# The order of all steps of a planned kernel comes from a stored string, and two-bank steps take neighbouring banks

## The chip, the cores and the metric

One core of a Trainium2 chip. The number is the device time of one execution in microseconds (us). The kernel before was run three times.

## The reference

An attention block with 32 inducing vectors, and a gated feed-forward layer on its result. With `B, N, C = 4, 12416, 128`, `M = 32`, `DFF = 1536`:

```python
def mab(q, kv):
    s = scale * (q @ kv.transpose(0, 2, 1))
    a = np.exp(s - s.max(-1, keepdims=True))
    a /= a.sum(-1, keepdims=True) + 1e-09
    return a @ kv
h = mab(I, x)                     # I: the inducing vectors, per batch
y = mab(x, h).reshape(B * N, C)
gate = np.maximum(y @ w_gate, 0.0)
out = (gate * (y @ w_val)) @ w_out
```

## The kernel before

Batch 0's first attention runs in `first_batch`, written out by hand. Everything after it is a list of 1454 steps (`Op`): 751 on TensorE, 216 on ScalarE, 344 on VectorE, 65 on GpSimd, 78 on the sync engine. A step has a name, an engine, a duration that the planner assumes, the steps that it depends on, a number of PSUM banks that it takes or frees, and a function that emits its instructions. `Plan.order` lays the steps out in time by that model; the kernel then emits them in that order, so that each engine receives its instructions in the planned order and works through them in that order. The waits in the program come from the tiles that the instructions read and write, not from the planner.

What a batch b consists of:

- `prepare` (b = 1 to 3): `ld` loads of x (GpSimd queue), `turn` transposes (TensorE, with `xT` copies on VectorE, or by DMA on the sync queue for the pairs in `BY_DMA`), `s1a`/`s1b` scores, `p1` exponentials (ScalarE), `ha`/`hb` sums over tokens, `hs`, `hsum`, `zs` to `hT` small steps.
- `second_scores`: `S` scores against h, copied out by `Sc` (VectorE).
- `tables`: `g1`/`g2` gates, products `U` (VectorE), tables `T` (TensorE, 24 matmuls a step) and their copies `Tc`, and the same for `u5`, `T5`.
- `quadratic`: 48 `e` scores (TensorE, two matmuls of 512 columns), each with one exponential `f` of 128x1024 (ScalarE) into a ring of six `F` buffers of four; 48 output tiles `o`, each in two halves a and b. A unit is three tiles: `o..a` of its first takes two banks; a reciprocal `r` and a product `d` (VectorE, into `osb`) read both banks, and `d` frees them; every second unit is stored (`st`). There are 16 units in a batch, 64 in all.
- `check`: `far` sums of squares on GpSimd, `v`, `diag`, `vp`, `eps`, then `test`, twelve small GpSimd instructions. At the very end `tot`, `totp`, `left` and `load` turn the four tests into the condition of the branch to a general kernel.

PSUM has eight banks. Banks 0 to 3 are two double ones for `e`, `s1` and the like ("E"). Banks 4 to 7 are four single ones ("D"), numbered 0 to 3. A step that needs two D banks gets the two that came free first, whichever they are, and addresses them with

```python
def dbanks(o):
    a, b = o.got
    return AL[:, 4 + a : 5 + b : b - a, :]
```

In the plan of the kernel before, 113 steps take two banks: 40 of them (0,1) or (2,3), 27 (1,2), and 46 a pair with a gap: 25 (0,3), 11 (0,2), 10 (1,3). Of the units, the first eight of batch 2 (o2.0 to o2.23) alternate between (0,1) and (2,3); the last ten of batch 3 (o3.18 to o3.47) alternate between (1,3) and (0,2).

In the plan before, `pick` chooses at each moment, per engine, the step with the earliest latest start, by due times (`goal`, `LAG`) and boosts; exponentials come out in the order of their number.

Of the kernel before, what the change touches and what calls it, by code (L numbers as in the profile page):

```python
# [18 lines left out]
BOOST_FREE = 30.0  # L19
BOOST_PE = 6.0  # L20
# [8 lines left out]
BY_DMA = {(2, 1), (2, 3), (2, 5), (3, 1), (3, 3), (3, 5)}  # L29


class Op:
    __slots__ = (
        "name", "eng", "dur", "post", "deps", "emit", "take", "frees", "goal", "dma",
        "succ", "last", "start", "end", "seen", "got", "left", "first", "prev", "tail", "fixed", "boost",
# [3 lines left out]
class Plan:  # L39


    TOL = {"PE": 0.12, "ACT": 0.2, "DVE": 0.3}
    BANKS = {"E": 2, "D": 4}

# [3 lines left out]
    def op(self, name, eng, dur, emit, deps=(), post=None, take=None, frees=(), goal=1e9, dma=0.0):  # L48
# [10 lines left out]
        o.succ, o.got, o.fixed, o.boost = [], None, None, BOOST_FREE if o.frees and eng == 'DVE' else 0.0  # L59
# [11 lines left out]
    def order(self, begin):  # L71
        ops = self.ops
        for o in ops:
            for d, lat in o.deps:
                d.succ.append((o, lat))
            o.left = len(o.deps)
        for o in reversed(ops):
            o.last = o.goal - o.dur
            for s, lat in o.succ:
                o.last = min(o.last, s.last - self.lag(o, s, lat) - o.dur - o.dma)  # L80
        for o in ops:
            o.last -= o.boost
        free = dict.fromkeys(("PE", "ACT", "DVE", "POOL", "SP"), 0.0)
        free.update(begin)
        slots = {k: [0.0] * n for k, n in self.BANKS.items()}
        ready = {e: [] for e in free}
        for o in ops:
            if not o.left:
                ready[o.eng].append(o)
        server = free.pop("DMA", 0.0)  # L90
        done = []

        def est(o):
            if o.fixed is not None:
                return 0.0
            t = free[o.eng]
            for d, lat in o.deps:
                t = max(t, d.seen - d.post + self.lag(d, o, lat))
            if o.take:
                kind, n = o.take  # L100
                times = sorted(s for s in slots[kind] if s is not None)
                if len(times) < n:
                    return None
                t = max(t, times[n - 1])
            return t

        def pick(e):
            c = [(t, o) for o in ready[e] for t in [est(o)] if t is not None]
            if not c:
                return None  # L110
            base = min(t for t, _ in c)
            t, o = min(((t, o) for t, o in c if t <= base + 0.03), key=lambda a: a[1].last)
            tol = self.TOL.get(e)
            soon = [(u, v) for u, v in c if v.last < o.last and u < t + o.dur - tol] if tol else []
            if soon:
                u, v = min(soon, key=lambda a: a[1].last)
                fit = [(w, p) for w, p in c if w + p.dur <= u + tol]
                if fit:
                    t, o = min(fit, key=lambda a: a[1].last)
                else:  # L120
                    t, o = u, v
            return t, o

        while any(ready.values()):
            best = None
            for e in ready:
                p = pick(e)
                if p and (best is None or p[0] < best[0]):
                    best = p
            assert best, [(e, [o.name for o in r][:5]) for e, r in ready.items()]  # L130
            t, o = best
            ready[o.eng].remove(o)
            o.start = t
            o.end = t + o.dur
# [8 lines left out]
            if o.take:  # L143
                kind, n = o.take
                s = slots[kind]
                avail = sorted((i for i in range(len(s)) if s[i] is not None and s[i] <= t + 1e-9), key=lambda i: (s[i], i))
                o.got = sorted(avail[:n])
                assert len(o.got) == n
                for i in o.got:
                    s[i] = None  # L150
# [4 lines left out]
            for s, _ in o.succ:  # L155
                s.left -= 1
                if not s.left:
                    ready[s.eng].append(s)
        assert len(done) == len(ops)
        return sorted(done, key=lambda o: o.start)  # L160

# [9 lines left out]
def quadratic_body(ctx, tc, x, inducing, moe_w_gate, moe_w_val, moe_w_out, out):  # L171
# [390 lines left out]
    def prepare(b):  # L562
        s = state[b]
        s["turn"], s["load"] = {}, {}
        for q in (NQ, *range(NQ)):
# [13 lines left out]
            if q < NQ and (b, q) not in BY_DMA:  # L579
# [20 lines left out]
                s["turn"][q] = op(f"xT{b}.{q}", "DVE", 1.15, copy, frees=[o])  # L600
# [21 lines left out]
        for u in range(NQ // 2):  # L622
# [64 lines left out]
            def add(u=u, o=ha):  # L687
# [16 lines left out]
            [s["h"]],  # L704
        )
        zs = op(
            f"zs{b}", "DVE", 0.19,
# [4 lines left out]
            [hs],  # L712
        )
        o = op(f"zp{b}", "PE", 0.5, None, [zs], take=("D", 1))
        o.emit = lambda o=o: pe.matmul(dbank(o)[:, 0:M], ones32, small["zs"], start=True, stop=True)
        zc = op(
            f"zk{b}", "DVE", 0.15, lambda o=o: dve.tensor_copy(out=zk, in_=dbank(o)[:, 0:M]),
# [5 lines left out]
            f"h{b}", "DVE", 0.15,  # L723
# [7 lines left out]
            f"hc{b}", "DVE", 0.13,  # L731
# [7 lines left out]
                f"hT{b}", "DVE", 0.13,  # L739
# [5 lines left out]
    def second_scores(b):  # L745
# [5 lines left out]
        war = [*state[b - 2]["e_last"], state[b - 2]["far"]] if b >= 2 else []  # L751
        for u in range(4):
# [28 lines left out]
            d = op(f"Sc{b}.{u}", "DVE", 1.2 if u < 3 else 0.2, out_, war, frees=[o])  # L781
            s["Sd"].append(d)

        s["F5"] = []
        for v in range(2):
# [11 lines left out]
            o.emit = mm5  # L797
            k = len(f5_done)
# [18 lines left out]
    def tables(b):  # L817
# [23 lines left out]
        def gv(k):  # L841
# [9 lines left out]
            [o2],  # L851
# [9 lines left out]
        def value_out(to, lo, n):  # L861
# [7 lines left out]
        vw = op(f"vw{b}", "DVE", 0.33, lambda: value_out(M, 0, NS), [o2, *free_g])  # L869
        gw = op(f"gw{b}", "DVE", 0.33, lambda: gate_out(M, 0, NS), [m, *free_g])  # L870
        sc = op(
            f"sums{b}", "DVE", 0.15,
# [6 lines left out]
            f"mags{b}", "DVE", 0.5,  # L879
# [10 lines left out]
        def odd(src, dst):  # L890
            dve.tensor_copy(out=dst[:, :, 0 : G - 1], in_=src[:, :, 1:G])

        vo = op(f"vb{b}", "DVE", 0.4, lambda: odd(va, vb), [vv, vw])
        go = op(f"gb{b}", "DVE", 0.4, lambda: odd(ga, gb), [g, gw])
# [3 lines left out]
            f"u5a{b}", "DVE", 0.3,  # L898
# [6 lines left out]
            f"u5b{b}", "DVE", 0.3,  # L905
# [102 lines left out]
        def mm5(step, o):  # L1008
            ps = dbanks(o1_)

            def mm(k, half, t):
# [13 lines left out]
                f"T5c{b}", "DVE", 0.65,  # L1025
# [11 lines left out]
    def check(b):  # L1037
# [8 lines left out]
        for k in range(4):  # L1046
            part = flat[:, 768 * k : 768 * k + 768]
            steps.append((1.7, Z if k else A, part, part, mul))
            if k:
                steps.append((1.7, A, A, Z, add))  # L1050
# [4 lines left out]
        for k, (dur, dst, in0, in1, f) in enumerate(steps):  # L1055
# [13 lines left out]
            f"v{b}", "DVE", 0.5,  # L1069
# [10 lines left out]
            [vm],  # L1080
        )
        o = op(f"vp{b}", "PE", 0.6, None, [dg], take=("D", 1))
        o.emit = lambda: pe.matmul(dbank(o)[:, 0:P], ones32, diag, start=True, stop=True)
        ep = op(
            f"eps{b}", "DVE", 0.25,
            lambda: dve.tensor_reduce(out=eps, in_=dbank(o)[:, 0:P], axis=AX.X, op=ALU.max),  # L1086
            frees=[o],
        )
        lo = op(
            f"zlo{b}", "DVE", 0.13,  # L1090
            lambda: dve.tensor_reduce(out=small["zlo"], in_=zk, axis=AX.X, op=ALU.min),
            [s.get("zk")], goal=late,
        )
        hi = s["zcheck"] = op(
            f"zhi{b}", "DVE", 0.13,
# [25 lines left out]
    def quadratic(b):  # L1121
        s = state[b]
        s["e_last"], s["o_all"] = [], []
# [3 lines left out]
        def rest():  # L1127
# [11 lines left out]
            s["e_last"].append(o)  # L1139

            def exp(o=o):
# [7 lines left out]
                f"fr{b}", "ACT", 0.6, exp, state[b - 1].get("o_rest", []) if b else [],  # L1149
# [12 lines left out]
            def out2():  # L1162
# [16 lines left out]
                f"dr{b}", "DVE", 0.25,  # L1179
# [12 lines left out]
        def scores(xb):  # L1192
# [3 lines left out]
            for j in range(4):  # L1196
# [10 lines left out]
                if xb == NX - 1:  # L1207
                    s["e_last"].append(o)
# [8 lines left out]
        units = {}  # L1217

        def outputs(p):
# [48 lines left out]
            if tt == TPB - 1:  # L1268
                f_done[k] = [o2]
# [86 lines left out]
    for o in plan.ops:  # L1356
        if o.eng == "PE" and o.take is None and not o.name.startswith("e"):
            o.boost = BOOST_PE
        if o.name.startswith("r"):
            o.boost = BOOST_FREE  # L1360
# [253 lines left out]
```

## Time and profile before

| what | value |
|---|---|
| median of 3 runs | 370.79 us (367.03 to 372.0) |
| profiled execution, its own time | 374.55 us |
| its span | 372.8 us |
| mean granted TensorE clock | 0.905 of 2.4 GHz |
| busy: TensorE, ScalarE, VectorE, GpSimd | 280.8, 216.3, 181.2, 86.9 us |

The span runs from the first to the last instruction of the profiled execution; 1.75 us of its own time lie around it. It is 1.0% above the median of the runs. Busy time of TensorE counts the last part of a matmul's passage through the array too, so that it is not work at its peak.

### The profile page before, as it was taken

How to read it: one execution, taken by the hardware profiler on the slowest of the kernel's cores; microseconds unless marked ns; L12 is line 12 of the kernel's file. 1: busy time of each engine (PE TensorE's matmuls, PEld its weight loads, DVE VectorE, ACT ScalarE, POOL GpSimd, SP SyncE). 2: the span in 40 equal slices, each digit the busy share in tenths (PEclk: the TensorE clock that was granted, in tenths of full speed). 3: DMA queues.
4: the chain of work that ended last, by engine and by line, in shares of the span. 5: the costliest groups of instructions: out<-in, count | busy, mean ns of one | idle time of the engine just before them, and what ended most of it. 6: DMA issues, size and time to landing. Idle time of an engine off the chain costs nothing.

```text
span 372.8 us, 15723 instructions
## 1 busy us (share of the span) xinstructions
PE 280.8 (75%) x7251; PEld 208.8 (56%) x7251; DVE 181.2 (49%) x383; ACT 216.3 (58%) x248; POOL 86.9 (23%) x146
## 2 busy tenths in 40 slices
PE   5796889874779687778758889997878878767740
PEld 2672577664456465446637558876555657544430
DVE  4559856550337922344224796642368443432330
ACT  3456887952668154677522996785558454548600
POOL 3663076002300050080101007600020500061011
PEclk9699899995789998999957999998789999989985
DMA  8999963318972412252534443440202204422230
GB/s 302 384 158 215 212 126 155 156 44 196 214 164 86 122 28 86 86 142 96 142 62 130 151 96 60 169 184 4 88 2 86 88 4 191 160 84 86 88 152 28
DMA packets 30042, 46.85 MB, mean 126 GB/s; under 512 B 16624, under 2 KB 17296, under 8 KB 29968
## 3 DMA queue, kind: packets, MB, share of 16 engines
q1 hardware_dynamic: 25056, 35.04, 26.7%
q0 software_dynamic: 4864, 10.72, 15.8%
q8 instruction: 58, 0.95, 1.1%
q14 instruction: 16, 0.13, 0.1%
q10 hardware_dynamic: 48, 0.02, 0.0%
HBM read 27.80 MB, written 25.43 MB: 143 GB/s over the span
## 4 chain that ended last, share of the span: by engine, by line
PE 62%; DVE 17%; ACT 10%; issue 7%; POOL 1%; DVEq 0%; POOLq 0%; ACTq 0%
PE AL L1257 32%; ACT F L1211 9%; PE AL L1201 9%; DVE osb L1290 7%; PE AL L977 6%; PE AL L664 2%; PE AL L631 2%; DVE S L777 2%; DVE xT L596 2%; PE xT_ps L372 2%; PE AL L586 1%; DVE rzo L1285 1%; DVE U L933 1%; PE warm_ps L290 1%; PE AL L1012 1%
## 5 line engine op out<-in xcount | busy, mean ns | idle before, releaser
L1211 ACT ACTIVATE F<-AL 128x1024 f16<-128x1024 f32 x192 | 184.5, 1031 | 100.8 <-PE AL L1201 96.7
L1257 PE MATMUL AL<-T,F 64*128 64x129 f16 x3456 | 148.7, 228 | 30.0 <-DVE osb L1290 20.9
L1257 PEld LDWEIGHTS <-F 64*128 64x128 f16 x3456 | 115.5, 99 | 65.3 <-issue 33.9
L1201 PE MATMUL AL<-S,pairs 64*128 64x512 f16 x384 | 77.8, 402 | 14.0 <-ACT F L1211 11.2
L1290 DVE TENSOR_TENSOR osb<-AL,rzo 128x768 f32<-128x768 f32 x64 | 61.0, 954 | 8.7 <-PE AL L1257 7.6
L1285 DVE RECIPROCAL rzo<-AL 128x6 f32<-128x6 f32 x64 | 12.4, 195 | 102.7 <-PE AL L1257 94.7
L1061 POOL TENSOR_TENSOR far<-S 128x768 f16<-128x768 f16 x16 | 25.6, 1610 | 137.9 <-DVE U L933 81.4
L1201 PEld LDWEIGHTS <-pairs 64*128 64x128 f16 x384 | 23.3, 97 | 26.9 <-issue 22.8
L977 PE MATMUL AL<-wo,U 64*128 64x128 f16 x768 | 25.8, 216 | 4.1 <-DVE osb L1290 1.5
L977 PEld LDWEIGHTS <-U 64*128 64x128 f16 x768 | 22.9, 94 | 9.0 <-issue 5.9
L1061 POOL TENSOR_TENSOR far<-far 128x768 f16<-128x768 f16 (+2 forms) x20 | 25.0, 1249 | 1.6
L242 POOL DMA_DIRECT2D x<-in_x_dram x18 | 9.8, 555 | 50.2 <-PE AL L664 39.9
L596 DVE COPY xT<-AL 128x2048 f16<-128x2048 f16 x12 | 14.7, 1221 | 7.5 <-PE AL L586 6.9
L1101 POOL TENSOR_SCALAR eps<-eps 128x1 f32<-128x1 f32 x4 | 0.8, 189 | 70.3 <-DVE eps L1086 58.9
L645 ACT ACTIVATE p<-AL 128x1024 f16<-128x1024 f32 x9 | 9.2, 1023 | 12.7 <-PE AL L631 12.5
L631 PE MATMUL AL<-indT,xT 64*128 64x32 f16 x576 | 11.1, 175 | 5.9 <-issue 5.4
L777 DVE CAST S<-AL 128x1024 f16<-128x1024 f32 x12 | 14.6, 1214 | 1.3 <-PE AL L765 1.3
L631 PEld LDWEIGHTS <-xT 64*128 64x128 f16 x576 | 9.5, 94 | 7.0 <-issue 6.6
L664 PE MATMUL AL<-p,x 64*128 64x32 f16 x576 | 10.1, 178 | 2.5 <-DVE osb L1290 1.4
L664 PEld LDWEIGHTS <-x 64*128 64x128 f16 x576 | 9.5, 96 | 4.2 <-issue 3.5
L373 DVE COPY xT<-xT_ps 128x1024 f16<-128x1024 f16 (+1 forms) x15 | 8.5, 582 | 6.5 <-PE xT_ps L372 6.3
L393 ACT ACTIVATE p1a<-s_ps 128x256 f16<-128x256 f32 (+2 forms) x16 | 5.2, 332 | 9.8 <-PE s_ps L391 9.7
(157 smaller groups left out, 263.9 us busy)
## 6 DMA issues: line engine op xcount, KB each, us to landing
out_dram<-osb SPq DMA_DIRECT2D x64, 384.0 KB, 2.9
x<-in_x_dram POOLq DMA_DIRECT2D x18, 512.0 KB, 11.6
x<-in_x_dram SPq DMA_DIRECT2D x9, 512.0 KB, 6.5
x<-in_x_dram SPq DMA_DIRECT2D x6, 256.0 KB, 7.9
wg<-in_moe_w_gate_dram POOLq DMA_DIRECT2D x1, 384.0 KB, 4.9
wv<-in_moe_w_val_dram POOLq DMA_DIRECT2D x1, 384.0 KB, 6.9
wo<-in_moe_w_out_dram POOLq DMA_DIRECT2D x1, 384.0 KB, 8.2
out_dram<-osr SPq DMA_DIRECT2D x4, 64.0 KB, 3.1
```

Source lines behind the costliest of these rows:

```text
L242: pool.dma_start(out=x16(b, t0, n), in_=xv[b][:, t0 : t0 + n, :])
L596: dve.tensor_copy(out=xTs[q].rearrange("p t (h j) -> p h t j", h=2), in_=ps)
L631: return pe.matmul(ps[:, k, t, :], xTs[qs[k]][ROWS[half], t, :], indT[ROWS[half], :], start=step == 0 and t == 0, stop=step == 1, skip_gro ...
L664: pe.matmul(ps[:, r, 0:M], l, m, start=k == 0 and t == 0, stop=k == 1, skip_group_check=True,)
L777: dve.tensor_copy(out=S[b % 2][:, gs[0] : gs[0] + 2, :], in_=dbanks(o))
L977: pe.matmul(ps[:, k, 0:P], U[js[k] % NU][r, i, t].rearrange("p k m -> p (k m)"), wo[r, t, :], start=(step, i, t) == (0, 0, 0), stop=(step, ...
L1061: pool.tensor_tensor(out=dst, in0=in0, in1=in1, op=f)
L1201: pe.matmul(ebanks(o)[:, r, :], pairs[ROWS[r], par, j, :], S[b % 2][ROWS[r], g, :], start=True, stop=True,)
L1211: lambda o=o, j=j: act.activation(out=dst[:, j], in_=ebanks(o), func=AF.Exp, scale=sm_scale,),
L1257: pe.matmul(ps[:, k_, :], l, m_, start=step == 0 and j == 0, stop=step == 1 and j == n - 1,)
L1285: lambda: dve.reciprocal(out=rzo[rr], in_=view()[:, :, :, P : P + 1]),
L1290: lambda: dve.tensor_tensor(out=dst[:, :, 3 * h6 : 3 * h6 + 3, :], in0=view()[:, :, :, 0:P], in1=rzo[rr].broadcast_to([P, 2, 3, P]), op=AL ...
```

## The change

The greedy choice in `Plan.order` goes. For each of the five engines a string (`ORDER`, two characters a step) says in which order its steps run; the planner only goes through the five lists and assigns banks. A step that takes n banks takes n neighbouring ones, the earliest free; on a tie the bank stored in `BANKS` decides (`NEAR`), and else the pair (1,2) is left last. Among the 113 two-bank steps `NEAR` names bank 0 for 30, bank 1 (the pair (1,2)) for 26, bank 2 for 26 and none for 31. Assumed durations are altered, and the planner is told of more of the dependencies that the tiles have; no step is added or dropped, none changes its engine, and no step's instructions change except by the banks that they address.

```diff
-BOOST_FREE = 30.0
-BOOST_PE = 6.0
-BY_DMA = {(2, 1), (2, 3), (2, 5), (3, 1), (3, 3), (3, 5)}
+BY_DMA = {(2, 3), (3, 3), (2, 1), (3, 1), (2, 5), (3, 5)}
+DIGITS = "0123456789abcdefghijklmnopqrstuvwxyzABCDEFGHIJKLMNOPQRSTUVWXYZ+-"
+SEQUENCES = [
+    [64 * DIGITS.index(s[i]) + DIGITS.index(s[i + 1]) for i in range(0, len(s), 2)] for s in ORDER
+]
+NEAR = ["-0123".index(c) - 1 for c in BANKS]
...
+    def banks(self, o, slots, t):
+        kind, n = o.take
+        s = slots[kind]
+        best = None
+        for b in range(len(s) - n + 1):
+            free = s[b : b + n]
+            if None in free:
+                continue
+            u = max(t, *free)
+            if best is None or u < best[0] - 1e-9:
+                best = (u, b)
+            elif u < best[0] + 1e-9 and (o.near == b or (n == 2 and best[1] == 1 and o.near != 1)):
+                best = (u, b)
+        return best
...
+        queue = {e: list(reversed(s)) for e, s in zip(self.ENGINES, sequences)}
         done = []
...
+        while len(done) < len(ops):
+            best = None
+            for e in self.ENGINES:
+                if not queue[e]:
+                    continue
+                o = ops[queue[e][-1]]
+                if o.left:
+                    continue
...
-                o.got = sorted(avail[:n])
-                assert len(o.got) == n
+                o.got = list(range(got, got + n))
...
-                s["turn"][q] = op(f"xT{b}.{q}", "DVE", 1.15, copy, frees=[o])
+                s["turn"][q] = op(f"xT{b}.{q}", "DVE", 1.22, copy, frees=[o])
...
-        war = [*state[b - 2]["e_last"], state[b - 2]["far"]] if b >= 2 else []
+        war = [*state[b - 2]["e_all"], state[b - 2]["far"]] if b >= 2 else []
...
-            if tt == TPB - 1:
-                f_done[k] = [o2]
+            f_done.setdefault(k, []).append(o2)
...
-                            [d], dma=1.03,
+                            halves[-2:], dma=1.03,
...
-    order = plan.order(BEGIN)
-    quadratic_body.plan = order
-    for o in order:
+    quadratic_body.plan = plan
+    for o in plan.order(BEGIN, SEQUENCES, NEAR):
```

What the strings say, decoded with the numbers of the steps:

- TensorE begins `S0.3 S0.0 S0.2 e0.2.2 S0.1 e0.3.1 turn1.0 e0.0.1 ...`. Batch 1's prepare (19 TensorE steps) stands at places 6 to 50 of the 751, before 14 to 149; batch 2's (16 steps) at 115 to 189, before 305 to 348; batch 3's at 261 to 373, before 405 to 532. `S1.0` stands ahead of the first output, `o0.0a`, which is at place 68 (before 48). `o3.0a` is at place 621 (before 612) with 30 `e` steps behind it.
- Units and exponentials no longer run in the order of their numbers (`f0.2.2 f0.3.1 f0.0.1 f0.1.2`; units 0, 1, 4, 5, 2, 3 in batch 0).
- Half b of an output tile follows directly on its own half a in 21 of 192 cases (before 43); in the others another step stands between them.
- VectorE ends `r3.14 tot d3.14 r3.12 d3.12 r3.13 d3.13 left`, TensorE `... o3.41a o3.41b totp`; `vp3` stands behind `o3.23b` and `eps3` behind `rr3`. Before, `eps3`, `tot`, `totp` and `left` came behind everything else.
- On the GpSimd queue `ld3.1 ld2.5 ld3.2 ld3.6 ld3.0` stand ahead of `far0`, and `ld3.4`, `ld3.5` behind `test0`; on the sync queue `turn2.3` stands ahead of the first store.

## Rows read from the trace of the kernel before

**Rows 1.** The page's busy time (share of the span) and instructions, two engines.
```profile
PE 280.8 (75%) x7251; PEld 208.8 (56%) x7251; DVE 181.2 (49%) x383; ACT 216.3 (58%) x248; POOL 86.9 (23%) x146
```

**Rows 2.** Groups of TensorE matmuls: busy us, mean ns, idle time before and its releasers.
```profile
L1257 PE MATMUL AL<-T,F 64*128 64x129 f16 x3456 | 148.7, 228 | 30.0 <-DVE osb L1290 20.9 <-DVE S L777 2.3 <-DVE rzo L1285 1.1
L1201 PE MATMUL AL<-S,pairs 64*128 64x512 f16 x384 | 77.8, 402 | 14.0 <-ACT F L1211 11.2 <-DVE S L777 1.9 <-ACT p L645 0.2
L977 PE MATMUL AL<-wo,U 64*128 64x128 f16 x768 | 25.8, 216 | 4.1 <-DVE osb L1290 1.5 <-DVE S L777 1.5 <-DVE xT L596 0.6
...
L664 PE MATMUL AL<-p,x 64*128 64x32 f16 x576 | 10.1, 178 | 2.5 <-DVE osb L1290 1.4 <-issue 1.0
...
L765 PE MATMUL AL<-xT,hT 128*32 128x512 f16 x96 | 7.4, 384 | 4.4 <-DVE osb L1290 3.0 <-DVE hT L458 0.7 <-DVE T L996 0.5
```

**Rows 3.** Timeline, VectorE, the last units, on banks (1,3) and (0,2).
```profile
342.79 0.96 DVE L1290 TENSOR_TENSOR osb<-AL,rzo 128x768 f32<-128x768 f32 x1 [0.48 <-PE AL L1257]
...
357.62 0.96 DVE L1290 TENSOR_TENSOR osb<-AL,rzo 128x768 f32<-128x768 f32 x1 [0.48 <-PE AL L1257]
```

**Rows 4.** Timeline, TensorE, the same units.
```profile
354.94 1.97 PE L1257 MATMUL AL<-T,F 64*128 64x129 f16 x53 [1.03 <-DVE osb L1290]
357.19 0.41 PE L1257 MATMUL AL<-T,F 64*128 64x129 f16 x8 [0.28 <-DVE rzo L1285]
358.63 1.23 PE L1257 MATMUL AL<-T,F 64*128 64x129 f16 x28 [1.03 <-DVE osb L1290]
```

**Rows 5.** Timeline, VectorE, first and last of eight units on (0,1) and (2,3).
```profile
232.20 0.96 DVE L1290 TENSOR_TENSOR osb<-AL,rzo 128x768 f32<-128x768 f32 x1
...
246.46 0.96 DVE L1290 TENSOR_TENSOR osb<-AL,rzo 128x768 f32<-128x768 f32 x1
```

**Rows 6.** Timeline: one weight-load run and three matmul runs.
```profile
28.58 0.62 PE L765 MATMUL AL<-xT,hT 128*32 128x512 f16 x8 [0.66 <-DVE hT L458]
30.68 0.61 PE L1201 MATMUL AL<-S,pairs 64*128 64x512 f16 x4 [0.55 <-DVE S L777]
...
87.08 0.59 PE L664 MATMUL AL<-p,x 64*128 64x32 f16 x32
...
236.57 0.58 PEld L1257 LDWEIGHTS <-F 64*128 64x128 f16 x20 [0.18 <-PE AL L1257]
```

**Rows 7.** Busy us by stretch: length, PE, PEld, DVE, ACT, POOL, clock, DMA share, GB/s.
```profile
30.00:50.00 20.00, 15.26 (x309) 9.09 (x302) 17.50 (x35) 17.53 (x19) 4.25 (x6) 0.91 1.07 213
90.00:110.00 20.00, 13.65 (x259) 9.38 (x258) 5.44 (x16) 10.23 (x11) 4.18 (x15) 0.73 0.95 194
230.00:250.00 20.00, 18.85 (x555) 15.75 (x555) 10.83 (x21) 14.09 (x15) 8.44 (x8) 1.00 0.40 157
```

**Rows 8.** The stretch 230:250, matmuls of L1257, L1201 and L631 alone, in that order.
```profile
230.00:250.00 20.00, 16.32 (x454) 13.33 (x456) 1.00 0.40 157
230.00:250.00 20.00, 5.03 (x28) 1.54 (x26) 1.00 0.40 157
230.00:250.00 20.00, 1.30 (x64) 1.12 (x64) 1.00 0.40 157
```

**Rows 9.** Timeline of the end, all engines.
```profile
360.13 0.96 DVE L1290 TENSOR_TENSOR osb<-AL,rzo 128x768 f32<-128x768 f32 x1
361.00 0.28 DVE L1086 TENSOR_REDUCE eps<-AL 128x1 f32<-128x128 f32 x1
...
364.49 0.21 POOL L1116 TENSOR_TENSOR fine<-fine,c 128x12 f32<-128x12 f32 x1
...
365.57 0.16 DVE L1348 TENSOR_SCALAR left<-AL 128x1 int32<-128x1 f32 x1 [0.68 <-PE AL L1345]
```

**Rows 10.** Timeline, TensorE, inside batch 1's prepare.
```profile
93.94 0.22 PE L675 MATMUL AL<-ones,p 64*128 64x1 f16 x5 [4.68 <-issue]
```

**Rows 11.** The page's DMA queue of instructions: packets, MB, share of 16 engines.
```profile
q8 instruction: 58, 0.95, 1.1%
```

**Rows 12.** Groups of ScalarE: the exponentials.
```profile
L1211 ACT ACTIVATE F<-AL 128x1024 f16<-128x1024 f32 x192 | 184.5, 1031 | 100.8 <-PE AL L1201 96.7
```

More of the change, by code (lines that the diff above doesn't have):

```diff
@@ L32 @@
+NEAR = ["-0123".index(c) - 1 for c in BANKS]
 class Op:
     __slots__ = (
-        "name", "eng", "dur", "post", "deps", "emit", "take", "frees", "goal", "dma",
-        "succ", "last", "start", "end", "seen", "got", "left", "first", "prev", "tail", "fixed", "boost",
+        "name", "eng", "dur", "post", "deps", "emit", "take", "frees", "goal", "dma", "near",
+        "succ", "last", "start", "end", "seen", "got", "left", "prev", "first", "tail", "fixed", "boost", "index",
     )
 class Plan:
-    TOL = {"PE": 0.12, "ACT": 0.2, "DVE": 0.3}
@@ L58, in op @@
         o.deps += [(f, None) for f in o.frees]
-        o.succ, o.got, o.fixed, o.boost = [], None, None, BOOST_FREE if o.frees and eng == 'DVE' else 0.0
+        o.succ, o.got, o.fixed, o.near = [], None, None, -1
+        o.index = len(self.ops)
         self.ops.append(o)
@@ L74, in order @@
             for d, lat in o.deps:
-                d.succ.append((o, lat))
+                d.succ.append(o)
             o.left = len(o.deps)
[L77 to L83, printed above, removed]
+        for o, b in zip(ops, near):
+            o.near = b
@@ L84, in order @@
+        free = dict.fromkeys(self.ENGINES, 0.0)
         free.update(begin)
         slots = {k: [0.0] * n for k, n in self.BANKS.items()}
[L86 to L89, printed above, removed]
         server = free.pop("DMA", 0.0)
+        queue = {e: list(reversed(s)) for e, s in zip(self.ENGINES, sequences)}
         done = []
[L93 to L119, printed above, removed]
-                else:
-                    t, o = u, v
-            return t, o
@@ L124, in order @@
[L124 to L134, printed above, removed]
+        while len(done) < len(ops):
[6 more added lines that the diff above has]
+                    continue
+                t, got = free[e], None
+                if o.fixed is not None:
+                    t = 0.0
+                else:
+                    for d, lat in o.deps:
+                        t = max(t, d.seen - d.post + self.lag(d, o, lat))
+                if o.take:
+                    found = self.banks(o, slots, t)
+                    if not found:
+                        continue
+                    t, got = found
+                if best is None or t < best[0]:
+                    best = (t, o, got)
+            t, o, got = best
+            queue[o.eng].pop()
+            o.start, o.end = t, t + o.dur
@@ L154, in order @@
             done.append(o)
-            for s, _ in o.succ:
+            for s in o.succ:
                 s.left -= 1
[L157 to L160, printed above, removed]
+        return done
 def quadratic_kernel(tc, x, inducing, moe_w_gate, moe_w_val, moe_w_out, out):
```

157 lines of the change are left out of this document (109 added, 48 removed).

## The prediction

> **What bounds the kernel now.** I read the busy shares first [rows 1]: TensorE 75%, ScalarE 58%, VectorE 49%, so no engine is full over the span, and the question is which waits leave the fullest one idle. The groups of TensorE name them [rows 2]: the largest is the output matmuls' wait for `d`, the product that frees two banks, 20.9 us; the same wait stands before S (3.0), T (1.5) and the token sums (1.4), 26.8 us together. Busy time flatters TensorE, so I counted its work from the distance at which matmuls follow each other. Output matmuls: 20 weight loads in 0.58 us, 0.029 each [rows 6]; 3456 of them [rows 2] make 100.2 us. Scores: four in 0.61 us, of which the last pair takes the 0.40 that one lasts, so 0.21 a pair or 0.105 each [rows 2, 6]; 384 make 40.3. Table matmuls, 768 of the outputs' width at 0.029: 22.3. Small ones: 32 in 0.59 us of which the last takes 0.18, 0.0132 each [rows 2, 6]; the source has 2076 after the first batch (576 `s1`, 582 and 150 in the sums, 384 transposes, 192 for T5, 192 gates): 27.4. S by its busy time 7.4 [rows 2]; 48 matmuls of e5 at 0.105, 5.0; the rest, an estimate, 5. Sum 208 us. The planned part runs from 28.6 [rows 6] to the end of the last output matmul at 359.9 [rows 4], 331 us: TensorE works 63% of it. In the best stretch, 230 to 250, the same prices give 454 x 0.029 + 28 x 0.105 + 64 x 0.0132 = 16.9 of 20 us, 85% [rows 8], with no other engine near its limit [rows 7].
>
> The Trainium skill (Perfetto Trace Analysis, Identifying the Most-Contended Engine) says that matmul busy time is no measure of how near TensorE is to its limit and that weight-load time is better. Here 75% busy stands against 56% weight load and my 63% [rows 1], so the trace agrees. With busy time as work, 280.8 us at the best stretch's 94% [rows 7] would put the floor at 280.8 / 0.94 = 299 us of span instead of the 282 that rival C below has.
>
> **The change part by part.** *Neighbouring banks.* The last ten units of the kernel before use (1,3) and (0,2). There `d` waits 0.48 us after its reciprocal for TensorE, which meanwhile does eight matmuls of the next unit, in the other two banks; TensorE then stands 1.03 us until `d` is over [rows 3, 4]. Two units that share no bank thus wait for each other in both directions: I take it that a slice with a gap counts as all banks from its first to its last. From 342.79 to 357.62 four intervals pass [rows 3], 3.71 us a unit. Eight units on (0,1) and (2,3) take seven intervals from 232.20 to 246.46 [rows 5], 2.04 us a unit, although the `r` and `d` work is the same. With neighbours only, two units without a common bank have no slice that overlaps. What goes is at least the 26.8 us of TensorE idle, if nothing else is late there. Next late are the exponentials: a unit uses three of 1.03 us [rows 12], 3.1 us when they keep no stock; in the last batch 30 of 48 are still to come when outputs begin.
>
> *The order of prepare.* Before, batches 2 and 3 were transposed and scored late in the previous batch, in a lump; batch 1's is partly such a lump too. The stretch 90 to 110 is one: TensorE busy 13.65, ScalarE 10.23, VectorE 5.44 of 20, granted clock 0.73 [rows 7]. The small matmuls cannot run beside their own exponentials, and few others were left to fill in. The new lists spread these steps over places 6 to 50, 115 to 189 and 261 to 373, among scores and outputs. The price: the first output stands at place 68 instead of 48. Before, the stretch 30 to 50 already had VectorE 17.50 and ScalarE 17.53 of 20 busy [rows 7]; batch 1's copies go into it now, so the first output comes later, and the kernel must win this back at the three transitions and at the end. That is why I don't use the best stretch's 85% for the whole part.
>
> *Halves.* A half b directly behind its half a waits; the load before `b` shows 0.18 us [rows 6]. 43 such cases become 21: 22 x 0.18 = 4 us at most, inside the rate below.
>
> *The end.* The last `d` ends at 361.09; `eps`, twelve GpSimd steps, `tot`, `totp` and `left` follow one another until 365.73 [rows 9]. In the new lists `vp3` stands with 24 output tiles (eight units) behind it, and only `totp` and `left` follow the last outputs. `totp` runs beside the last `r` and `d`. 365.73 - 361.09 - 0.2 for `left` = 4.4 us go. Cover: eight units of at least 2.04, 16 us, over a chain of 3.4 on GpSimd; without it the 4.4 stay. The 7.1 us from `left` to the end of the span are kept.
>
> *Queues.* On GpSimd five loads of batches 2 and 3 pass `far0`, and wait for the sums of batch 1 that free their buffers; `far0` and `test0` queue behind them. Nobody needs `far0` until `v0`, some eight units later. Two loads now wait behind `test0`. On the sync queue `turn2.3` passes the first store; it waits for its load and S1.0, both due before the first store is. I take 0 for all, between a gain of 1 and a loss of 5 us (one stall of a prepare, [rows 10]), and 0 is nearest to what both queues show. Assumed durations and added dependencies of the planner emit nothing: 0.
>
> *The sum.* The rate of the planned part decides. Bounds: 63% (nothing gained) and 85% (all as in the best stretch). I take the middle, 74%: 208 / 0.74 = 281 us. Then 28.6 + 281 + 1.2 (last matmul to end of `d`, 359.9 to 361.1) + 0.2 + 7.1 + 1.75 around the span = 319.9 us, against 374.55 of the profiled execution. The median of the runs is 370.79, factor 0.990: 317 us.
>
> **The rivals.**
> *B, only waits and tail go.* The fixed order meets durations that vary, each engine stands at its next step though another is ready, and the interleaving gains nothing: 374.55 - 26.8 - 4.4 = 343.4, times 0.990 = 340. For it: an in-order list can't react, and VectorE is full at the beginning [rows 7]. Against it: before, the order was fixed too, and the transitions have the most room.
> *C, the best stretch everywhere.* 208 / 0.85 = 245, 283.6 in all, 281. For it: all engines' work would fit. Against: the beginning is VectorE's, and the end has outputs alone.
> *D, the middle pair.* A unit on (1,2) leaves no second pair, so the next unit waits for its `d`: 3.71 instead of 2.04, 1.67 us. Between 26 (named) and 57 (with those that name none) of the two-bank steps may get it: 319.9 + 43 to + 95 = 363 to 415, or 360 to 411. It makes the kernel slower by 2% from (382 - 320) / 1.67 = 37 such steps. For it: with three pairs instead of six the choice is narrower. Against: (1,2) was used 27 times before, and the planner lays every bank wait out before it is emitted, and fills it with other steps.
> *E, instructions come late.* In batch 1's prepare TensorE stood 4.68 us with nothing to wait for that the profile shows [rows 10]. Instructions arrive in 58 packets of 0.95 MB together [rows 11], 16 KB each; 7251 matmuls and as many loads [rows 1] make 65 bytes an instruction, so a prepare of about 650 matmuls is five packets. If each of 15 stalled 4.68 us, 70 us would be added: 390, or 386; slower by 2% from 13 stalls. For it: batch 1's prepare moves to where the DMA share is 1.07 [rows 7], and small matmuls use instructions fastest. Against: spread among outputs and scores they are used more slowly, and stalls of this kind are part of the 63% already.
> The Trainium skill (Runtime: NRT & Kernel Launch, Instruction fetch mechanics) says that instructions come in blocks of 16 KiB by a DMA queue of the engine's own and that this is mostly hidden. The size agrees with [rows 11]; [rows 10] shows a gap that may be such a fetch. By the page this rival adds nothing; by the row 4.68 us for each.
>
> That the change does nothing is excluded: the lists and the pairs differ, and each engine takes its instructions in order.
>
> **How the numbers follow.** My forecast has 0.55, with its own range from 80% (260 us, 298.9, 296) to 335, where B begins. B 0.20 (335 to 348), C 0.10 (below 296), D 0.08 (0.05 of it slower by over 2%, 0.03 within), E 0.07 (0.02 faster, 0.04 within, 0.01 slower). The range 295 to 346 leaves out C's lower part, D, E and the end of B, 2 in 10. Two per cent, 7.4 us, is about what a measurement of this kernel can tell from no change. Faster 0.55 + 0.20 + 0.10 + 0.02 = 0.87, within 0.03 + 0.04 = 0.07, slower 0.05 + 0.01 = 0.06.
>
> **What would show it.** Right: no `d` that waits for TensorE 0.48 us after its reciprocal, and the wait of matmuls for `d` well under 26.8 us; units of the last batch 2 to 3 us apart; no stretch of 20 us after 60 with TensorE under 14 busy; the last `d` about 0.3 us before `left`. Wrong: long idle of TensorE for `xT`, hacc or `d` on a unit of (1,2), "issue" gaps in the first 60 us (E), or VectorE as what ends the waits far beyond the beginning, which would mean that the rate of 74% is out of reach.

## The result, and the profile after

The new kernel takes 300.5 us (median of 4 runs, 299.82 to 304.33) against 371.39 before: a ratio of 0.811, with 95% between 0.804 and 0.818. Some executions of either kernel fall in a slower state; ratios, and differences from the kernel before, leave those out. The forecast was 317. The profiled execution took 300.5 us, its span is 298.5.

The page's busy times of the kernel after, as in [rows 1]:
```profile
PE 255.7 (86%) x7251; PEld 201.6 (68%) x7251; DVE 186.8 (63%) x383; ACT 215.0 (72%) x248; POOL 84.6 (28%) x146
```
The same 7251 matmuls, 74 us less span. TensorE's own busy time fell by 25 us. Its mean granted clock rose from 0.905 to 0.94; how much of the 25 us is due to that, and how much to matmuls that follow each other more closely, was not worked out.

The groups of TensorE matmuls after, as in [rows 2] (L1312, L1257, L1033, L718 and L819 are L1257, L1201, L977, L664 and L765 of before):
```profile
L1312 PE MATMUL AL<-T,F 64*128 64x129 f16 x3456 | 134.7, 219 | 5.4 <-issue 3.6 <-DVE xT L650 0.2
L1257 PE MATMUL AL<-S,pairs 64*128 64x512 f16 x384 | 75.0, 387 | 2.0 <-ACT F L1266 1.2 <-DVE S L831 0.5
L1033 PE MATMUL AL<-wo,U 64*128 64x128 f16 x768 | 29.1, 227 | 1.0 <-issue 1.0
L718 PE MATMUL AL<-p,x 64*128 64x32 f16 x576 | 10.8, 176 | 3.9 <-issue 3.8
L819 PE MATMUL AL<-xT,hT 128*32 128x512 f16 x96 | 7.4, 384 | 2.7 <-DVE hT L794 2.2 <-DVE SR L833 0.5
```
No group waits for `d` (osb) any more. The idle time before output matmuls fell from 30.0 to 5.4 us, that before scores from 14.0 to 2.0. What is left is mostly "issue": no releaser that the profile shows.

Busy us by stretch, columns as in [rows 7]: to the first unit's reciprocal, then to those of the 17th, the 33rd and the end of the last `d`:
```profile
28.50:74.60 46.10, 34.35 (x1078) 25.79 (x1080) 30.73 (x59) 26.41 (x28) 15.04 (x29) 0.81 0.85 162
74.60:144.10 69.50, 60.60 (x1881) 47.05 (x1877) 45.85 (x90) 48.21 (x53) 19.21 (x27) 0.98 0.67 157
144.10:207.50 63.40, 58.06 (x1811) 47.03 (x1807) 40.93 (x86) 53.03 (x57) 15.74 (x24) 0.97 0.36 115
207.50:290.50 83.00, 80.95 (x2156) 65.47 (x2152) 54.03 (x111) 74.94 (x81) 18.71 (x37) 1.00 0.38 147
```
From 207.5 on TensorE is busy 98% and ScalarE 90%; at the prediction's prices its 1664 output, 154 score, 192 table matmuls and about 3 us of others are 73 of 83 us, 88% of work, more than the 85% of the best stretch of before. The start is the weak part: about 27 of 46 us by the same prices, 58%, at a granted clock of 0.81. There is one weak stretch after it, around batch 2's prepare:
```profile
100.00:120.00 20.00, 13.85 (x583) 11.86 (x585) 9.99 (x23) 9.94 (x11) 1.18 (x2) 0.91 0.55 143
```

The end, as in [rows 9]:
```profile
289.54 0.96 DVE L1344 TENSOR_TENSOR osb<-AL,rzo 128x768 f32<-128x768 f32 x1
290.41 0.15 DVE L1403 TENSOR_SCALAR left<-AL 128x1 int32<-128x1 f32 x1
```
`left` ends 0.06 us after the last `d`, before 4.6 us after it.

### The profile page after: what moved, and what is told of

The parts are those of the page before. It is cut to its first block, busy times and chain, and to the rows that moved or that the text cites. A ratio compares the mean times of both kernels' runs of the same rounds, so it can differ in the third digit from the quotient of the medians.

```text
span 298.5 us, 15634 instructions
## 1 busy us (share of the span) xinstructions
PE 255.7 (86%) x7251; PEld 201.6 (68%) x7251; DVE 186.8 (63%) x383; ACT 215.0 (72%) x248; POOL 84.6 (28%) x146
## 4 chain that ended last, share of the span: by engine, by line
## 5 line engine op out<-in xcount | busy, mean ns | idle before, releaser
L1266 ACT ACTIVATE F<-AL 128x1024 f16<-128x1024 f32 x192 | 184.1, 1030 | 45.2 <-PE AL L1257 43.8
L1312 PE MATMUL AL<-T,F 64*128 64x129 f16 x3456 | 134.7, 219 | 5.4 <-issue 3.6
L1312 PEld LDWEIGHTS <-F 64*128 64x128 f16 x3456 | 108.0, 95 | 32.5 <-PE AL L1312 18.6
L1257 PE MATMUL AL<-S,pairs 64*128 64x512 f16 x384 | 75.0, 387 | 2.0 <-ACT F L1266 1.2
L1117 POOL TENSOR_TENSOR far<-S 128x768 f16<-128x768 f16 x16 | 23.4, 1467 | 84.4 <-DVE U L989 83.8
L1339 DVE RECIPROCAL rzo<-AL 128x6 f32<-128x6 f32 x64 | 12.5, 196 | 47.7 <-PE AL L1312 47.1
L1033 PE MATMUL AL<-wo,U 64*128 64x128 f16 x768 | 29.1, 227 | 1.0 <-issue 1.0
L1033 PEld LDWEIGHTS <-U 64*128 64x128 f16 x768 | 25.3, 100 | 5.1 <-issue 2.0
L1257 PEld LDWEIGHTS <-pairs 64*128 64x128 f16 x384 | 22.1, 95 | 6.1 <-issue 4.7
L718 PE MATMUL AL<-p,x 64*128 64x32 f16 x576 | 10.8, 176 | 3.9 <-issue 3.8
L718 PEld LDWEIGHTS <-x 64*128 64x128 f16 x576 | 9.9, 95 | 5.3 <-issue 4.7
## 6 DMA issues: line engine op xcount, KB each, us to landing
x<-in_x_dram POOLq DMA_DIRECT2D x18, 512.0 KB, 11.2
```

The source lines that it names most:

```text
L718: pe.matmul(ps[:, r, 0:M], l, m, start=k == 0 and t == 0, stop=k == 1, skip_group_check=True,)
L1033: pe.matmul(ps[:, k, 0:P], U[js[k] % NU][r, i, t].rearrange("p k m -> p (k m)"), wo[r, t, :], start=(step, i, t) == (0, 0, 0), stop=(step, ...
L1117: pool.tensor_tensor(out=dst, in0=in0, in1=in1, op=f)
L1257: pe.matmul(ebanks(o)[:, r, :], pairs[ROWS[r], par, j, :], S[b % 2][ROWS[r], g, :], start=True, stop=True,)
L1266: lambda o=o, j=j: act.activation(out=dst[:, j], in_=ebanks(o), func=AF.Exp, scale=sm_scale,),
L1312: pe.matmul(ps[:, k_, :], l, m_, start=step == 0 and j == 0, stop=step == 1 and j == n - 1,)
```

## The experiments

The theory after the result: neighbouring pairs end a false wait between units that share no bank (about 27 us), the check leaves the end (4.5), and the rest, some 40 us, comes from the order, through the transitions between batches. The rivals: the pairs alone, the order alone, a stretch's own pace that has nothing to do with pairs; later, several ways in which the order could work.

**Old lists, neighbouring pairs (x1).** The new planner is given the lists of the kernel before, engine by engine. `NEAR` and one dependency that the new kernel adds are left out with the new lists, so what lies between this kernel and the new one contains them too.
```diff
-ORDER = ( ... )                     # the new lists
+ORDER = ( ... )                     # those of the kernel before
...
-            [s.get("zk"), state[b - 1]["check"] if b else None], goal=late,   # zlo
+            [s.get("zk")], goal=late,
...
-    for o in plan.order(BEGIN, SEQUENCES, NEAR):
+    for o in plan.order(BEGIN, SEQUENCES):
```


> The lists of the kernel before, engine by engine, go through the new planner, which gives each two-bank step a neighbouring pair; only the pairs differ from the kernel before (and where a step is emitted among those of other engines). My theory (bank waits and order each carry a part): the 26.8 us of TensorE idle for d go and little else, 371.4 - 26.8 = 345, between 335 and 352; the lumps of prepare and the tail stay. Rival 1 (the order does it all): 365 to 372. Rival 2 (the pairs do it all): 300 to 310.

Measured: 342.29 us, 0.931 of before (0.919 to 0.943). Two groups of its TensorE matmuls, and two of TensorE's waits (total us, times, longest us):
```profile
L1312 PE MATMUL AL<-T,F 64*128 64x129 f16 x3456 | 138.3, 222 | 9.2 <-DVE S L831 2.7 <-DVE osb L1344 1.6 <-issue 1.0
L1257 PE MATMUL AL<-S,pairs 64*128 64x512 f16 x384 | 74.3, 386 | 15.4 <-ACT F L1266 12.4 <-DVE S L831 1.9 <-ACT p L699 0.3
```
```profile
PE AL L819 <- DVE osb L1344: 2.2, 3, 1.3
...
PE AL L1033 <- DVE osb L1344: 1.1, 1, 1.1
```
The wait of outputs for `d` falls from 20.9 to 1.6 us, that of all matmuls from 26.8 to 4.9; the scores' wait for exponentials (ACT F), 11.2 before, stays at 12.4. The theory holds: pairs carry 7%, neither nothing nor all.

**New lists, pairs with gaps (x2).** After planning, banks 1 and 2 are exchanged.
```diff
+        PHYS = (0, 2, 1, 3)
+        for o in done:
+            if o.take and o.take[0] == "D":
+                o.got = sorted(PHYS[i] for i in o.got)
         return done
```


> The new kernel, with banks 1 and 2 of the four exchanged after planning: (0,1) becomes (0,2), (2,3) becomes (1,3). Lists, plan and real conflicts over banks are the same, only the slices have gaps. My theory: all 64 units wait for each other's d again, at most 3.71 - 2.04 = 1.67 us each, 107 us, less what other steps between fill: 350 to 400, with d waiting about 0.5 us for TensorE and TensorE about 1 us for d. Rival (the order does it all): 299 to 306.

Measured: 401.35 us, 1.087 of before (1.075 to 1.099): 101 us more than the new kernel, and slower than the old one. The four added lines shift its line numbers by 4. Its outputs as a group:
```profile
L1316 PE MATMUL AL<-T,F 64*128 64x129 f16 x3456 | 155.5, 226 | 60.7 <-DVE osb L1348 40.9 <-DVE rzo L1343 6.1 <-DVE xT L654 5.6
```
A piece of its timeline, among batch 3's units (start, us, engine, line, operation; in brackets the idle time before it and what ended it):
```profile
343.97 0.41 PE L1316 MATMUL AL<-T,F 64*128 64x129 f16 x8 [0.29 <-DVE rzo L1343]
...
344.40 0.96 DVE L1348 TENSOR_TENSOR osb<-AL,rzo 128x768 f32<-128x768 f32 x1 [0.48 <-PE AL L1316]
...
345.41 0.76 PE L1316 MATMUL AL<-T,F 64*128 64x129 f16 x20 [0.82 <-DVE osb L1348]
```
The same pattern as in [rows 3, 4]: eight matmuls of a unit in other banks, `d` waits 0.48 us for them, then TensorE 0.82 for `d`. Lists, plan and true conflicts over banks are those of the new kernel, so the slice with a gap is the cause. The wait is in the program as it is built: 50 of the 64 `d` wait for a semaphore that a matmul into the bank between their two sets, and in the new kernel's program none of the 64 has a wait for TensorE of its own beside that of its reciprocal. Whether the chip by itself would hold up such a step was not tried. The rival that the order does it all is out.

**The kernel before, banks 1 and 2 exchanged (x3).** The same four lines at the end of the old `order`; steps on (0,1) and (2,3) get gaps, those on (0,2) and (1,3) lose them, and the 25 on (0,3) keep theirs. So 65 of the 113 two-bank steps have a gap, where before 46 had one.
```diff
+        PHYS = (0, 2, 1, 3)
+        for o in done:
+            if o.take and o.take[0] == "D":
+                o.got = sorted(PHYS[i] for i in o.got)
```

> The kernel before, with banks 1 and 2 exchanged after planning. The first eight units of batch 2, on (0,1) and (2,3) before, get gaps, the last ten of batch 3 lose them. My theory: the pace follows the gaps: units of batch 2 go from 2.04 to 3.2 us or more, the last ones from 3.7 to under 3.0; in all 362 to 385, as gains and losses about cancel. Rival (the pace comes from the stretch, with its exponentials and its end, not from the pairs): both paces stay as they were, 367 to 373.

Measured: 380.79 us, 1.032 of before (1.018 to 1.046). Timeline, VectorE: units of batch 2, now on gaps, and the last of batch 3, now on neighbours:
```profile
243.12 0.96 DVE L1294 TENSOR_TENSOR osb<-AL,rzo 128x768 f32<-128x768 f32 x1 [0.48 <-PE AL L1261]
246.38 0.96 DVE L1294 TENSOR_TENSOR osb<-AL,rzo 128x768 f32<-128x768 f32 x1 [0.48 <-PE AL L1261]
...
266.47 0.96 DVE L1294 TENSOR_TENSOR osb<-AL,rzo 128x768 f32<-128x768 f32 x1
...
356.00 0.96 DVE L1294 TENSOR_TENSOR osb<-AL,rzo 128x768 f32<-128x768 f32 x1
...
367.28 0.96 DVE L1294 TENSOR_TENSOR osb<-AL,rzo 128x768 f32<-128x768 f32 x1
```
Eight units of batch 2 take 23.35 / 7 = 3.34 us each, against 2.04 in [rows 5]. The last six take 11.28 / 5 = 2.26, against 3.47 before (342.79 to 360.13 in [rows 3, 9]). The pace moves with the gaps and not with the stretch. The times go with their number too: none with a gap takes 342.3 us (x1), 46 take 369.9 (the kernel before, measured beside it), 65 take 380.8, which is 0.60 and 0.59 us a gap. In the new order 112 gaps cost 101 us, 0.90 each.

**Greedy planner with neighbouring pairs (x4).** The old `pick`, with old durations and due times; only the choice of banks is new.
```diff
-                times = sorted(s for s in slots[kind] if s is not None)
-                if len(times) < n:
-                    return None
-                t = max(t, times[n - 1])
+                s = slots[kind]
+                times = [
+                    max(s[i : i + n]) for i in range(len(s) - n + 1) if None not in s[i : i + n]
+                ]
+                if not times:
+                    return None
+                t = max(t, min(times))
...
```


> The greedy planner of the kernel before, old durations and due times, but choosing only neighbouring pairs. It may order steps a little otherwise than before. My theory: like the old lists with neighbours, 335 to 352; the other 35 to 50 us of the change are the searched order's. Rival (a correct bank rule is all that the planner lacked): 300 to 315.

Measured: 342.78 us, 0.928 (0.916 to 0.941): the same as the old lists with neighbours. A right bank rule is worth 7% to this planner, and the lists' 42 us lie beyond it.

**The check back at the end (x5).** In the new lists, `vp3` goes to the place before `totp`, `eps3` and `tot` to the places before `left` (two characters a step; the first list is TensorE's, the second VectorE's, each from the change on).
```diff
-        "jWjXlkkEjYkFkGkOkHkIlmkJiKm2k1k2lAmqlBlClOlDlElalFlbm4lcmoldlekWlfkXkYmkkZk+mmlsk-ltlul+lv"
-        "lwm0mwlxmxmylKmzmAlQmgmBmhlMmimjmsmtlSlTlUlVlWm6lXm7m8m9mambmH"
+        "jWjXlkkEjYkFkGkOkHkIlmkJm2k1k2lAmqlBlClOlDlElalFlbm4lcmoldlekWlfkXkYmkkZk+mmlsk-ltlul+lvlw"
+        "m0mwlxmxmylKmzmAlQmgmBmhlMmimjmsmtlSlTlUlVlWm6lXm7m8m9mambiKmH"
...
-        "kliIjZiJj+kKkLk3iLk4lGlHlglhiNl0l1lylzmCmDmumGmvlYlZmcmdmI"
+        "kliIjZiJj+kKkLk3k4lGlHlglhiNl0l1lylzmCmDmumvlYlZmcmdiLmGmI"
```

> The new kernel, with the last batch's vp3, eps3, test and tot put back behind all outputs, as before. My theory: the chain from eps to left that stood behind the last d before (361.1 to 365.7) comes back, 300.5 + 4.5 = 305, between 303.5 and 306.5. Rival (the last stores end as late as the check, so that the tail is worth nothing): 299.5 to 301.5.

Measured: 305.43 us, 0.827 (0.822 to 0.831): 4.9 us more than the new kernel, as expected. The timeline of its end:
```profile
289.50 0.96 DVE L1344 TENSOR_TENSOR osb<-AL,rzo 128x768 f32<-128x768 f32 x1
290.37 0.28 DVE L1142 TENSOR_REDUCE eps<-AL 128x1 f32<-128x128 f32 x1
...
293.87 0.21 POOL L1172 TENSOR_TENSOR fine<-fine,c 128x12 f32<-128x12 f32 x1
...
294.96 0.16 DVE L1403 TENSOR_SCALAR left<-AL 128x1 int32<-128x1 f32 x1 [0.68 <-PE AL L1400]
```
The last `d` ends where it did; `left` ends 4.6 us later.

**Prepare early, in the greedy plan (x9).** To the greedy planner with neighbours:
```diff
+    early = ("turn", "xT", "s1", "p1", "ha", "hb", "hs")
+    for o in plan.ops:
+        if o.name.startswith(early):
+            o.boost += 30.0
```


> The greedy planner with neighbouring pairs, and 30 us taken off the due times of all steps of prepare, which moves them to places 5 to 82, 187 to 313 and 378 to 504 of TensorE's list (from 14 to 149, 305 to 348 and 405 to 532). My theory (the lump of prepare late in a batch is what the searched order removes): about half of the 42 us between greedy with neighbours and the new kernel, 315 to 330. Rival (the rest comes from the fine order of scores, outputs and tables): 336 to 346.

Measured: 373.12 us, 0.999 of before (0.994 to 1.005), about 29 us worse than without the boost. Two of its TensorE waits (total us, times, longest):
```profile
PE AL L1207 <- ACT F L1217: 13.5, 30, 1.0
PE AL L771 <- DVE osb L1296: 7.8, 6, 1.4
```
My theory that the lump of prepare is what the new order removes falls in this form: the spread alone doesn't help, the scores wait for exponentials as before, and second scores now queue behind `d`. Why it loses so much wasn't taken further.

**Tables early; both early (x11).** The same edit for second scores, the small steps to `hT` and all of `tables`, by 15 us; then 25 us for these and 10 for prepare.
```diff
+    tables_ = ("zs", "zp", "zk", "rz", "h1", "h2", "h3", "hc", "hT", "S", "g", "on", "v", "U", "u5", "T", "rel")
+    for o in plan.ops:
+        if o.name.startswith(early):
+            o.boost += 0.0              # 10.0 in the second
+        elif o.name.startswith(tables_) and o.name[:2] not in ("v0", "v1", "v2", "v3", "vp"):
+            o.boost += 15.0             # 25.0 in the second
```

> The greedy planner with neighbouring pairs, and 15 us off the due times of second scores and tables of all batches (prepare as it falls out): when the first table matmuls of batches 1 to 3 come, 9, 6 and 12 outputs of the batch before are left, instead of 0, 0 and 9. Theory (the transitions are long since tables run with no outputs beside them): 320 to 336. Rival (only an order tuned step by step brings it): 338 to 350, and after the early prepare that lost 30 us, slower than 350 is possible too, if early table products hold up the products d on VectorE.

> The same with 10 us off the due times of prepare and 25 off those of second scores and tables: 15, 15 and 21 outputs of the batch before are left at the first table matmul, 28, 27 and 27 at the first token sums. Theory (transitions): 315 to 332, less than with tables alone. Rival (step by step): 338 to 350; slower than 350 if VectorE holds up the products d.

Measured: 339.39 us, 0.914 (0.905 to 0.924), and 340.29, 0.917 (0.907 to 0.926). That is 3.4 and 2.5 us less than the greedy planner with neighbours. The end of the first of the two:
```profile
327.64 0.96 DVE L1296 TENSOR_TENSOR osb<-AL,rzo 128x768 f32<-128x768 f32 x1
328.51 0.15 DVE L1354 TENSOR_SCALAR left<-AL 128x1 int32<-128x1 f32 x1
```
In both plans the check no longer stands behind the outputs, which in the new lists is worth 4.9 us (x5). So moving whole groups of steps brought nothing beyond that. Of the explanations on trial an order tuned step by step is the one left, but no run shows it by itself.

**No loads of batch 3 (x8).** One line:
```diff
-    f"ld{b}.{q}", "POOL", 0.9, lambda b=b, q=q: load_x(b, q), [war],
+    f"ld{b}.{q}", "POOL", 0.9, (lambda b=b, q=q: load_x(b, q)) if b < 3 else None, [war],
```


> The new kernel without the seven loads of batch 3's x: its steps use what batches 1 and 2 left in those buffers, so batch 3's output is of other data. Theory A (instruction blocks wait behind the loads on the GpSimd queue): the 3.8 and 0.8 us in which TensorE stands without a releaser near 110 to 116 go, with part of those before 60, and the clock stays up: 293 to 298. Rival B (prepare's small matmuls use up instructions faster than blocks come, loads or not): the gaps stay, 298.5 to 301.5.

Measured: 297.67 us (297.26 to 297.83), 2.8 less than the new kernel. TensorE's stops without a releaser between 96 and 125 us:
```profile
PE AL L729 <- issue: 1.9, 2, 1.6
...
PE AL L718 <- issue: 0.8, 1, 0.8
```
They fall from 4.6 us (3.8 and 0.8) to 2.7: shorter, not gone. A stop of 4.0 us stands at 54, where the new kernel had 2.64 at 50, so that over the whole span they fall only from 17.3 to 14.8. Both theories hold in part.

**No loads of batches 2 and 3 (x13).** The same with no load at all after batch 1's.
```diff
-    f"ld{b}.{q}", "POOL", 0.9, lambda b=b, q=q: load_x(b, q), [war],
+    f"ld{b}.{q}", "POOL", 0.9, None, [war],
```

> The new kernel without any loads of x of batches 2 and 3 (their steps use what batch 0 and 1 left in the buffers, so these two batches' output is of other data). It bounds what the loads cost in any order. Theory A: all stops without a releaser after 42 us go, 288 to 295. Theory B: stops of 1 to 4 us stay in the prepare of batches 1, 2 and 3: 295 to 300.

Measured: 291.68 us (288.9 to 292.92). The three longest stops without a releaser before 70 us, in its timeline:
```profile
40.43 0.44 PE L640 MATMUL AL<-eye,x 64*128 64x64 f16 x18 [1.49 <-issue]
...
48.49 0.44 PE L718 MATMUL AL<-p,x 64*128 64x32 f16 x21 [0.94 <-issue]
...
52.22 0.41 PE L685 MATMUL AL<-indT,xT 64*128 64x32 f16 x19 [1.56 <-issue]
```
and the three longest of the new kernel before 60 us:
```profile
40.93 0.66 PE L640 MATMUL AL<-eye,x 64*128 64x64 f16 x18 [1.82 <-issue]
...
52.84 0.47 PE L718 MATMUL AL<-p,x 64*128 64x32 f16 x21 [2.64 <-issue]
...
56.57 0.44 PE L685 MATMUL AL<-indT,xT 64*128 64x32 f16 x19 [0.94 <-issue]
```
The loads are worth 8.8 us in all. The time is in theory A's range, but stops of up to 2.4 us stay, as theory B has it: over the whole span 11.1 us of them, against 17.3 with the loads.

What the stops are can be read from the packets of the instruction queue, 16 KB each. In the trace of the new kernel 12 stops are half a us or longer; each ends 1.2 to 1.6 us after such a packet has landed. The same holds for all 12 of the kernel before and all 8 of this one. The stop of 2.64 us ends at 52.84; the queue moves nothing from 46 to 50.4, and then, from 50.4 to 51.6:
```profile
q8 instruction: 1, 0.02, 4.9%
```
So TensorE stands for want of instructions. The late packets themselves take 0.9 to 1.3 us, so they were begun late; why, and how the loads have a part in it, no run shows.

**Two loads later; all loads later (x10, x12).** Only GpSimd's list is changed: `ld3.4` and `ld3.5` behind two steps of `far1`; then all loads of batches 2 and 3 that stood ahead of `far0.1` moved behind batch 1's last token sums and between the steps of `far0`. GpSimd's list in both:
```diff
-        "b55a5d5g5j5m5p58b0b2bagWbfgYgRgT10b7bcg-1112131415161718191gh1h46U6V6W6X6Y6Z6+6-707178cJcK"
+        "b55a5d5g5j5m5p58b0b2bagWbfgYgRgT10b7bcg-1112131415161718191g6U6Vh1h46W6X6Y6Z6+6-707178cJcK"
...
-        "b55a5d5g5j5m5p58b0b2bagWbfgYgRgT10b7bcg-1112131415161718191gh1h46U6V6W6X6Y6Z6+6-707178cJcK"
+        "5a5d5g5j5m5p58gYb2b7b5ba10bfbcb01112gTgWgR1314g-15161718191gh1h46U6V6W6X6Y6Z6+6-707178cJcK"
```

> The new kernel, with ld3.4 and ld3.5 behind the first two steps of far1 on the GpSimd queue, so that they are under way after batch 2's prepare and not beside it. Theory A (instruction blocks wait behind loads): the 3.8 us gap near 112 goes, 295 to 299. Rival B (small matmuls alone): 300 to 301. Rival C (turn3.5, which stands ahead of batch 1's stores on the sync queue, now holds them up): 302 to 308.

Measured: 300.27 us, 0.811 (0.807 to 0.816), as the new kernel. The stops between 96 and 125 us fall to 2.6, others elsewhere rise: in all 19.5 us, against 17.3.

> The new kernel with another order of loads on the GpSimd queue alone: none of batch 2 or 3 starts before the last token sums of batch 1 (about 63 us), and then they come between the steps of far0. Theory A (TensorE's stops in batch 1's prepare come from instruction blocks that wait behind these loads, and the half clock from 58 to 72 from the stops): the 2.6 us stop at 50 and most of the half clock go, first reciprocal of a unit at 66 to 70 instead of 74.6, 293 to 298 in all. Theory B (small matmuls use blocks up faster than they come, loads or not): 299.5 to 301.5. Rival C (the loads are now late for batch 2's transposes, or meet its prepare): 302 to 310.

Measured: 305.95 us, 0.826 (0.820 to 0.832), slower than the new kernel by 5. The busy times of the new kernel's stretch from 42 us to its first unit, and of this kernel's:
```profile
42.00:74.60 32.60, 25.27 (x796) 20.13 (x793) 20.16 (x40) 17.95 (x19) 11.89 (x13) 0.76 0.75 140
```
```profile
42.00:70.00 28.00, 21.23 (x785) 16.90 (x779) 21.23 (x39) 17.43 (x19) 10.24 (x14) 0.94 0.44 82
```
The stretches in them at the lower of the clock's two levels (0.50, 1.2 of 2.4 GHz), two of the new kernel and one of this:
```profile
40.90:44.20 3.30, 3.27 (x54) 2.01 (x55) 2.54 (x5) 0.86 (x1) 0.00 (x0) 0.50 1.12 211
47.70:61.30 13.60, 10.03 (x316) 8.94 (x314) 5.98 (x12) 6.03 (x6) 1.06 (x2) 0.50 0.55 102
```
```profile
52.20:55.50 3.30, 2.72 (x61) 2.47 (x63) 0.43 (x1) 1.02 (x1) 0.00 (x0) 0.50 0.03 5
```
Its timeline at the first outputs' stores:
```profile
94.47 0.28 PE L1312 MATMUL AL<-T,F 64*128 64x129 f16 x3 [2.45 <-issue]
...
95.06 0.96 DVE L1344 TENSOR_TENSOR osb<-AL,rzo 128x768 f32<-128x768 f32 x1 [4.55 <-DMA out_dram<-osb]
...
96.07 0.45 PE L1215 MATMUL AL<-T,FR 64*128 64x129 f16 x5 [1.31 <-DVE osb L1344]
```
Theory A's first half came true: the stop of 2.64 us is gone (stops of 1.0 and 1.6 us stand there, for 2.64 and 0.94), the granted clock of the stretch is 0.94 instead of 0.76, and the first unit comes 4.4 us earlier (70.2 for 74.6). But the half clock lies at 47.7 to 61.3, not at 58 to 72 as expected, and it began 2.5 us before the stop at 50.2; so that stop didn't bring the clock down. Then more than this is given back: from its first to its 17th unit this kernel takes 78.0 us, the new one 69.5. Of these 8.5 us, TensorE's stops without a releaser are 6.0 (12.2 against 6.2). The loads also meet the stores of the first outputs: `d` waits 4.55 us for a store that is to free its `osb`, of which 1.31 reach TensorE. The time is in rival C's range, but most of the loss is stops that moved with the loads, not loads that came late.

## Why the prediction was right

*Direction and mechanism.* The wait that the trace named first was the right one. False waits between pairs with gaps: forecast 26.8 us, measured 27.6 (old lists with neighbours, 342.3, against 369.9 for the kernel before, measured beside it). In the traces TensorE's waits for `d` fall by 21.9, from 26.8 to 4.9; that the total comes so near is in part luck. What I took from the rows alone, that a slice with a gap counts as all that lies between, is what both exchanges of banks show, as a wait that the program holds. The 1.67 us a unit between the two paces bound what x2 lost: 107 us for 64 units, measured 101.

*The end.* 4.4 us forecast, 4.9 measured (x5).

*The rate.* The term that was mis-sized is the middle, 74%. The part from 28.6 to the last output matmul, at 289.2, takes 260.6 us: 208 / 260.6 = 80%. So 28.6 + 260.6 + 1.3 + 0.1 + 7.9 + 2.0 = 300.5: 20.4 us less than my 281, and 1 us more around the end. The 74% was only the middle between two bounds, worked out from nothing else, so that 317 came as near as it did is luck as much as reading. I had put the price of the fuller start on VectorE. It has 30.7 of 46.1 us there, TensorE stops without a releaser and the granted clock is 0.81. And I had not believed that anything could hold above 85%: the last 83 us hold 88%. The 299 us that busy time as work would give as a floor were just met (span 298.5), by chance: busy time isn't a fixed amount of work, it fell from 280.8 to 255.7.

*A wait that I didn't price.* Scores that wait for a free double bank (ACT F) cost 11.2 us before [rows 2], 12.4 in the old lists with neighbours, 1.2 after. Only the new order takes it away. Halves without a step between: the wait of output weight loads for TensorE's own last half falls from 24.7 us (122 times, old lists with neighbours) to 18.6 (95), 6.1 where I had 4 at most; the wait is also more frequent than the 43 cases that I counted.

*The transitions.* That they would shrink was right: from the first to the last unit's reciprocal the old lists with neighbours take 55.7 to 324.7, 269 us, the new ones 74.6 to 289.3, 215 us, although the first comes 19 us later. That it is the lump of prepare, or of tables, was my reading, and three plans with these moved earlier don't bear it out. What the experiments show is that the order as a whole gives 42 us with 4.9 of them at the end; which steps give the other 37 stays open. Where they are saved can be read: from the old lists with neighbours to the new ones the spans differ by 38.1 us, of which TensorE's busy time is 12.9 (268.6 to 255.7) and its idle time the rest; there the scores' wait for exponentials gives 11.2 us, all waits for copies of S 5.6 (6.1 to 0.5), for `d` 4.9 and for `tot` 4.7. One sign that I named for being right failed: the stretch 100 to 120 has TensorE busy 13.85 us, under 14, with a stop of 3.84 in it.

*The rivals.* B had the size of the pairs and the end right, but the order did bring more. D fell by its own condition: the plan uses (1,2) for one of 113 two-bank steps; a bank that `NEAR` names counts only on ties. E had the mechanism right and the size wrong: TensorE's stops are late instructions (x13), and its sign is there, stops of 1.82, 2.64 and 0.94 us before 60. But as before 12 of the 58 packets came late, and the stops take 17.3 us in all, 18.3 before, where E had 70 us more. Why they didn't grow was not tested.

## What to carry to other kernels

Look at which addresses a slice spans, not only at which it touches: if two tiles that share nothing wait for each other, exchange their banks and see whether the wait moves with them. A planner that doesn't know such a wait gives plans that the program can't keep; here a rule that makes it impossible was enough (x4). Beyond that, moving groups of steps by hand brought nothing here but the earlier check, and only the whole order did; the pace that the best stretch of a trace shows is a fair first bound for what such an order can reach, and not a ceiling.

## What was not expected of the hardware

Two batches of loads on the GpSimd queue cost 8.8 us (x13), though none of TensorE's waits of 0.2 us or more in the new kernel names one of them: with them TensorE's stops for want of instructions come to 17.3 us, without them to 11.1. Of 58 packets of instructions 46 cost no such stop of half a us; the other 12 cost 0.5 to 3.8 us each. In the new kernel the granted clock goes to the lower of its two levels, 1.2 and 2.4 GHz, right behind the stop of 1.82 us (40.9 to 44.2), as behind those of 3.84 and 2.38 (116.0 to 119.3, 180.9 to 184.1); but its longest stretch there, 47.7 to 61.3, began before the stop of 2.64 at 50.2. Placing loads elsewhere (x10, x12) moved the stops and didn't remove them.
